# Sums of the first batch's exponentials on TensorE, weight and row stores issued by SyncE and ScalarE, and gate products placed inside the next stage

## The chip, the cores and the metric

The kernel runs on one core of one Trainium2 chip. The time is that of one execution on the device, in microseconds (us), as the median of the runs shown. The profile is of one execution taken by the hardware profiler; a second trace of the changed kernel is compared with it further down.

## What is computed

The reference is an attention with a soft cap, a feed-forward layer, and a mixture of eight experts with capacity routing, in float32:

```python
scores = cap * np.tanh(scale * q @ k.T / cap)             # 4 batches, 12 heads, 448 rows, head size 64
attn   = np.exp(scores - scores.max(-1)); attn /= attn.sum(-1) + 1e-9
x      = attn @ v                                         # 1792 tokens x 768
x      = np.maximum(x @ w_in, 0) ** 2 @ w_out             # 768 -> 2048 -> 768
logits = x @ w_gate                                       # 8 experts
# tokens in falling order of their logits; each expert takes at most 224
out[mask_e] = np.maximum(x[mask_e] @ w1[e], 0) @ w2[e]
```

What this case is about is the sum of the exponentials below the fraction bar, the way of w_in and w_out into the core, and the products with w_gate.

## The kernel before, in words

**Attention** goes batch by batch and, in a batch, by six pairs of heads (`hp`). A pair's exponentials are in four tiles `p`: three of 128 keys for both heads (128x2x448) and one of the last 64 keys of each head (128x448, the upper half for the one head, the lower half for the other). TensorE makes the scores (L230, L232), ScalarE tanh and exp (L234, L235), TensorE the products with `v` (L255, L258). For the denominator GpSimd adds the tiles to one tile `z` (L241, L243, L247 twice), and TensorE sums `z` over its partitions by two products with a tile of ones (`norm`, L263). VectorE adds a small number (L265, for batch 0; ScalarE for the others), takes the reciprocal (L266) and multiplies (L268).

**The feed-forward layer** is three products per tile, since each operand is a high and a low part (`wh`, `wl`, `xh`, `xl`, `gh`, `gl`): `hidden` (L390 to L392) makes 16 tiles per batch, `output` (L440 to L442) six tiles of four weight pieces each. The weights arrive as 64-bit words. For batch 0 a piece is loaded to `raw` (L319, two buffers), decoded by three VectorE instructions (L323, L324, L325) into `wf` (three buffers) and stored to a cache in HBM by GpSimd's queue (L342); later batches load from the cache (L344). `split_weights` makes `wh` on ScalarE (L351) and `wl` on VectorE or GpSimd (L352). `gate_decode` does the same with 24 tiles `wt` of the transposed w_out (store at L486). `finish` transposes a result tile (L418) and stores rows of it (L421); `gate` makes six small products with w_gate (L429), VectorE copies them to `lt` (L460), `logits` transposes that (L475).

**The order.** `merge` takes steps from several generators, always from the one that stands furthest back by the costs that it yields. Stages: attention(0); hidden(0) with attention(1); output(0) and hidden(1) with attention(2); output(1) and hidden(2) with attention(3) and gate_decode; hidden(3) with gate_weights; output(3), output(2), routing and the experts. From the third stage on TensorE's instructions run as they are written. On the other engines the scheduler orders them by its own timeline, so that parts of gate_decode stand well ahead of the stage in which they are written. An instruction that waits holds up all that stand behind it on its engine, and a DMA's issue waits on the issuing engine for the data that it stores. PSUM has two buffers each of `big`, `acc` and `aux`; `aux` serves L255 (`U`), L263, L418, L429 and L475.

## Time and profile before

| | us |
|---|---|
| median of 3 runs (lowest to highest) | 1237.92 (1237.11 to 1242.08) |
| the profiled execution's own time | 1232.37 |
| its span in the trace | 1230.1 |
| TensorE busy | 1113.3 (91%) |
| GpSimd busy | 618.1 (50%) |
| VectorE busy | 680.0 (55%) |

By stage, from windows of the trace (PEclk is the granted TensorE clock, as a share of full speed):

| stage | window, us | TensorE busy | VectorE busy | GpSimd busy | PEclk | DMA share |
|---|---|---|---|---|---|---|
| attention(0) | 5 to 87 | 70.25 of 82 | 56.20 | 50.86 | 0.92 | 0.55 |
| hidden(0), attention(1) | 87 to 194 | 103.69 of 107 | 84.50 | 72.78 | 0.97 | 0.51 |
| output(0), attention(2) | 194 to 307 | 99.71 of 113 | 93.53 | 68.44 | 0.97 | 0.65 |
| hidden(1), end of attention(2) | 307 to 400 | 78.33 of 93 | 69.99 | 29.64 | 0.91 | 0.73 |
| output(1), hidden(2), attention(3) | 400 to 585 | 183.21 of 185 | 85.26 | 50.20 | 1.00 | 0.32 |
| hidden(3), gate_weights | 585 to 660 | 73.84 of 75 | 16.04 | 29.87 | 1.00 | 0.49 |
| output(3) to the experts' end | 660 to 1225 | 504.26 of 565 | 273.42 | 314.21 | 0.92 | 0.42 |

Where TensorE is busy for all of a window at a clock of 1.00, nothing but its own work sets the length. Where it isn't, a wait ended last, and a lower clock beside it makes the work after the wait longer. GpSimd's busy time leaves out the time in which it stands at a DMA's issue.

### The profile page before, as it was taken

How to read it: one execution, taken by the hardware profiler on the slowest of the kernel's cores; microseconds unless marked ns; L12 is line 12 of the kernel's file. 1: busy time of each engine (PE TensorE's matmuls, PEld its weight loads, DVE VectorE, ACT ScalarE, POOL GpSimd, SP SyncE). 2: the span in 40 equal slices, each digit the busy share in tenths (PEclk: the TensorE clock that was granted, in tenths of full speed). 3: DMA queues.
4: the chain of work that ended last, by engine and by line, in shares of the span. 5: the costliest groups of instructions: out<-in, count | busy, mean ns of one | idle time of the engine just before them, and what ended most of it. 6: DMA issues, size and time to landing. Idle time of an engine off the chain costs nothing.

```text
span 1230.1 us, 16798 instructions
## 1 busy us (share of the span) xinstructions
PE 1113.3 (91%) x6170; PEld 869.5 (71%) x6170; DVE 680.0 (55%) x1018; ACT 571.3 (46%) x873; POOL 618.1 (50%) x442
## 2 busy tenths in 40 slices
PE   5899989997797999999999988888797998898997
PEld 1236655665475777677788877777696898898997
DVE  5858879797778534444213446655577763323220
ACT  4787756452374744576563211222232434444542
POOL 4767576665332322222443423436665766766663
PEclk8999989998898999999999987997798988999999
DMA  7433654668777334222651322234344545555551
GB/s 259 151 116 114 213 187 156 211 206 268 265 240 241 112 117 120 90 77 78 205 180 44 101 67 67 76 100 163 121 140 151 159 141 183 193 187 180 191 188 36
DMA packets 70641, 187.35 MB, mean 152 GB/s; under 512 B 8416, under 2 KB 13824, under 8 KB 70560
## 3 DMA queue, kind: packets, MB, share of 16 engines
q1 hardware_dynamic: 55376, 150.48, 38.4%
q0 software_dynamic: 9536, 32.82, 7.4%
q10 hardware_dynamic: 5648, 3.00, 0.9%
q8 instruction: 48, 0.79, 0.2%
q14 instruction: 33, 0.27, 0.1%
HBM read 156.38 MB, written 29.88 MB: 151 GB/s over the span
## 4 chain that ended last, share of the span: by engine, by line
PE 39%; DVE 9%; issue 2%; ACT 1%; POOL 1%; DMA 1%; POOLq 0%; SPq 0%; ACTq 0%; DVEq 0%
PE big L829 9%; PE acc L800 8%; PE acc L440 4%; PE acc L441 3%; PE acc L442 3%; DVE wl L352 3%; PE aux L629 2%; PE acc L390 2%; PE acc L391 2%; PE acc L392 2%; DVE oh L699 2%; PE aux L526 1%; ACT wh L351 1%; PE aux L705 1%; PE acc L746 1%
## 5 line engine op out<-in xcount | busy, mean ns | idle before, releaser
L352 POOL TENSOR_TENSOR wl<-wf,wh 128x768 fp32r<-128x768 f32 (+1 forms) x156 | 268.6, 1725 | 230.5 <-ACT wh L351 227.0
L351 ACT CAST wh<-wf 128x768 fp32r<-128x768 f32 (+1 forms) x238 | 177.8, 747 | 389.4 <-PE acc L441 156.5
L800 PE MATMUL acc<-xs,wh 128*128 128x224 f32 x732 | 143.3, 300 | 32.7 <-DVE gh L816 31.3
L440 PE MATMUL acc<-gh,wh 128*128 128x448 f32 x384 | 158.0, 412 | 0.0
L442 PE MATMUL acc<-gh,wl 128*128 128x448 f32 x384 | 147.0, 383 | 11.2 <-POOL wl L352 10.5
L800 PEld LDWEIGHTS acc<-xs,wh 128*128 128x128 f32 x732 | 124.8, 213 | 36.1 <-DVE gh L816 34.7
L390 PE MATMUL acc<-xh,wh 128*128 128x448 f32 x384 | 147.8, 387 | 0.0
L352 DVE TENSOR_TENSOR wl<-wf,wh 128x768 fp32r<-128x768 f32 (+1 forms) x82 | 96.6, 1178 | 90.8 <-ACT wh L351 90.6
L441 PE MATMUL acc<-gl,wh 128*128 128x448 f32 x384 | 146.6, 382 | 0.0
L391 PE MATMUL acc<-xl,wh 128*128 128x448 f32 x384 | 140.6, 366 | 1.1 <-DVE xl L311 1.1
L392 PE MATMUL acc<-xh,wl 128*128 128x448 f32 x384 | 140.8, 367 | 0.0
L829 PE MATMUL big<-wh,gh 128*112 128x384 f32 x512 | 117.3, 341 | 0.0
L800 PE MATMUL acc<-xs,wl 128*128 128x224 f32 x366 | 107.4, 293 | 0.0
L234 ACT ACTIVATE p<-big,isc 128x896 f32<-128x896 f32 x96 | 86.3, 907 | 39.7 <-PE big L230 34.1
L390 PEld LDWEIGHTS acc<-xh,wh 128*128 128x128 f32 x384 | 72.3, 189 | 35.0 <-issue 19.2
L442 PEld LDWEIGHTS acc<-gh,wl 128*128 128x128 f32 x384 | 76.5, 199 | 21.7 <-POOL wl L352 12.7
L352 POOL TENSOR_TENSOR wl<-raw,wh 128x768 fp32r<-128x768 f32 x37 | 70.0, 1897 | 42.1 <-ACT wh L351 41.8
L235 ACT ACTIVATE p<-p,capt 128x896 f32<-128x896 f32 x96 | 89.7, 949 | 1.6
L440 PEld LDWEIGHTS acc<-gh,wh 128*128 128x128 f32 x384 | 76.6, 200 | 16.4 <-issue 11.0
L829 PEld LDWEIGHTS big<-wh,gh 128*112 128x112 f32 x512 | 86.6, 175 | 0.7
L266 DVE RECIPROCAL d<-d 128x448 f32<-128x448 f32 x24 | 70.8, 2949 | 26.1 <-ACT d L265 25.9
L243 POOL TENSOR_TENSOR z<-z,p 128x896 f32<-128x896 f32 x24 | 51.2, 2133 | 66.2 <-ACT p L235 65.6
(175 smaller groups left out, 1993.6 us busy)
## 6 DMA issues: line engine op xcount, KB each, us to landing
wf<-w SPq DMA_DIRECT2D x78, 384.0 KB, 3.3
raw<-w SPq DMA_DIRECT2D x50, 384.0 KB, 3.2
wf<-wi SPq DMA_DIRECT2D x48, 384.0 KB, 3.1
wf<-wo SPq DMA_DIRECT2D x72, 256.0 KB, 2.6
raw<-w_in SPq DMA_DIRECT2D x16, 768.0 KB, 5.2
raw<-w_out SPq DMA_DIRECT2D x24, 512.0 KB, 3.9
raw<-w_out_t SPq DMA_DIRECT2D x24, 512.0 KB, 4.9
qk<-qk SPq DMA_DIRECT2D x23, 480.0 KB, 5.5
```

The costliest lines, as they stand in the source:

```text
L234: nc.scalar.activation(p, ps[:, :n, :S], AF.Tanh, scale=self.isc)
L235: e = nc.scalar.activation(p, p, AF.Exp, scale=self.capt)
L351: nc.scalar.copy(wh[:, :w], wf[:, :w])
L352: low.tensor_sub(wl[:, :w], wf[:, :w], wh[:, :w].bitcast(F32))
L390: nc.tensor.matmul(ps, wh[:, d], xh, start=(d == 0), stop=False)
L391: nc.tensor.matmul(ps, wh[:, d], xl, start=False, stop=False)
L392: nc.tensor.matmul(ps, wl[:, d], xh, start=False, stop=(d == ND - 1))
L440: nc.tensor.matmul(ps, a, gh, start=(f == 0), stop=False)
L441: nc.tensor.matmul(ps, a, gl, start=False, stop=False)
L442: nc.tensor.matmul(ps, z, gh, start=False, stop=(f == NF - 1))
L800: nc.tensor.matmul(H[j], w[:, d], xs[:, d, x], start=(d == 0 and first), stop=(d == ND - 1 and last))
L829: nc.tensor.matmul(acc[h][:, s, :DM // 2], l, r[:, s * (DM // 2):(s + 1) * (DM // 2)], start=(j == 0 and first), stop=(j == NF2 - 1 and last))
```

## The change

For batch 0 alone GpSimd's additions are gone: `norm` accumulates, per pair of heads, six products with the tile of ones (three tiles, two heads) and one with a new 128x128 tile `duo`, which has ones in its two diagonal 64x64 blocks and so sums the last tile for both heads at once. The weight stores (16 of w_in, 24 of w_out, 24 of its transpose) and the load of `cap` go from GpSimd's queue to SyncE's. The row stores of batches 0 and 1 go from GpSimd's to ScalarE's queue. The gate products, the last tile's `finish` and the logits of batches 0 and 1 are put on a list `tail`, and the next hidden stage runs one of them after each of its first three tiles' products (`trailing`); output(3)'s last `finish` is run in output(2). The copy to `lt` goes to ScalarE, the transposes of `finish` stand behind the second quarter of the next tile's products instead of the first, except in output(2), and in batches 2 and 3 a step is yielded ahead of the last pair's `norm`.

```diff
--- before.py
+++ after.py
@@ -176,10 +176,14 @@
     def setup(self):
         nc, keep = self.nc, self.keep
         capt = keep.tile([128, 1], F32, name="capt")
-        nc.gpsimd.dma_start(capt, bass.AP(tensor=self.capv.tensor, offset=self.capv.offset, ap=[[0, 128], [1, 1]]))
+        nc.sync.dma_start(capt, bass.AP(tensor=self.capv.tensor, offset=self.capv.offset, ap=[[0, 128], [1, 1]]))
         self.capt = capt
         self.ones = keep.tile([128, DH], F32, name="ones")
         nc.vector.memset(self.ones, 1.0)
+        self.duo = keep.tile([128, 128], F32, name="duo")
+        nc.vector.memset(self.duo, 0.0)
+        for h in (slice(0, 64), slice(64, 128)):
+            nc.vector.memset(self.duo[h, h], 1.0)
         self.isc = keep.tile([128, 1], F32, name="isc")
         nc.vector.reciprocal(self.isc, capt)
         nc.vector.tensor_scalar(self.isc, self.isc, DH ** -0.5, None, op0=OP.mult)
@@ -198,6 +202,7 @@
         self.G = {}
         self.loaded = self.ready = 0
         self.x_t = {}
+        self.tail = []
         self.exps, self.norms = [], []
 
     def attention(self, b):
@@ -236,6 +241,8 @@
             if b == 0:
                 self.exps.append(e)
             P[hp, c] = p
+            if b == 0:
+                return
             if c == 1:
                 zs[hp] = z = ap.tile([128, 2, S], F32, name="z", bufs=2)
                 adder.tensor_add(z, P[hp, 0], p)
@@ -259,8 +266,15 @@
 
         def norm(hp):
             z = self.psum.tile([128, S], F32, name="aux")
-            for s in range(2):
-                nc.tensor.matmul(z[s * 64:s * 64 + 64], self.ones, zs[hp][:, s], start=True, stop=True)
+            if b == 0:
+                for c in range(KB):
+                    for s in range(2):
+                        nc.tensor.matmul(z[s * 64:s * 64 + 64], self.ones, P[hp, c][:, s],
+                                         start=(c == 0), stop=False, skip_group_check=True)
+                nc.tensor.matmul(z, self.duo, P[hp, KB][:, 0], start=False, stop=True, skip_group_check=True)
+            else:
+                for s in range(2):
+                    nc.tensor.matmul(z[s * 64:s * 64 + 64], self.ones, zs[hp][:, s], start=True, stop=True)
             d = ap.tile([128, S], F32, name="d", bufs=1)
             (nc.vector.tensor_scalar(d, z, self.eps, None, op0=OP.add) if b == 0 else nc.scalar.activation(d, z, AF.Identity, bias=self.eps))
             nc.vector.reciprocal(d, d)
@@ -290,7 +304,7 @@
                 if not whole:
                     yield 1.6
                 pv(hp - 1, 2, 4)
-                if not whole:
+                if not whole or hp == HP:
                     yield 1.6
                 norm(hp - 1)
                 yield 4.0 if whole else 0.8
@@ -339,7 +353,7 @@
             with self.after(self.norms, WAIT[0], n):
                 self.decode(wf, (self.wi if m == "i" else self.wo)[j], w)
             self.cache[m, j] = self.dram.tile([128, w], F32, name=f"w{m}{j}")
-            nc.gpsimd.dma_start(self.cache[m, j], wf[:, :w])
+            nc.sync.dma_start(self.cache[m, j], wf[:, :w])
         else:
             nc.sync.dma_start(wf[:, :w], self.cache[m, j])
         self.wtile[n] = (wf, w, nc.gpsimd if n >= self.at[NB - 1, "i"] or b == 0 and n % 6 else nc.vector, self.wts, 3)
@@ -392,6 +406,7 @@
                 nc.tensor.matmul(ps, wl[:, d], xh, start=False, stop=(d == ND - 1))
                 if d == 2:
                     yield 1.7
+            yield from self.trailing()
             r = mp.tile([128, S], F32, name="r", bufs=2)
             nc.scalar.activation(r, ps, AF.Relu)
             nc.scalar.activation(r, r, AF.Square)
@@ -402,6 +417,12 @@
             G.append((gh, gl))
             yield 1.7
 
+    def trailing(self):
+
+        if self.tail:
+            self.tail.pop(0)()
+            yield 1.5
+
     def output(self, b):
         nc, mp = self.nc, self.mp
         base = self.at[b, "o"]
@@ -418,7 +439,7 @@
                 nc.tensor.transpose(ps[:, c], xt[:, c * KP:(c + 1) * KP], self.c("ident"))
             o = mp.tile([KP, KC, 128], F32, name="rows", bufs=2)
             (nc.vector.tensor_copy if b == LAST and j == ND - 1 else nc.scalar.copy)(o, ps)
-            (nc.gpsimd if gated else nc.scalar).dma_start(
+            nc.scalar.dma_start(
                 rows[j // DA][b, :, :, j % DA * 128:(j % DA + 1) * 128], o)
             if b == LAST:
                 self.stored = j + 1
@@ -447,20 +468,29 @@
                         yield None
                     self.load_experts(-1)
                     yield from self.feed(0, 0)
-                if q == 0 and last is not None:
+                if q == int(b != LAST) and last is not None:
                     finish(*last)
                     yield 1.4
+                if j == 0:
+                    yield from self.trailing()
             xt = self.tp.tile([128, S], F32, name="xt")
             (nc.vector.tensor_copy if b == LAST and j == ND - 1 else nc.scalar.copy)(xt, ps)
             xts.append(xt)
             last = (j, xt)
-        if gated:
+        def gates():
+            nonlocal pl
             pl = self.psum.tile([128, S], F32, name="aux")
             gate(0, ND)
-            nc.vector.tensor_copy(lt, pl)
-            self.logits(b)
-        finish(*last)
-        yield 2.5
+            nc.scalar.copy(lt, pl)
+
+        pl = None
+        if gated:
+            self.tail += [gates, lambda: finish(*last), lambda: self.logits(b)]
+        elif b != LAST:
+            self.tail.append(lambda: finish(*last))
+        else:
+            finish(*last)
+            yield 2.5
 
     def gate_half(self, b):
         if b % 2 == 0:
@@ -483,7 +513,7 @@
             t = self.ap.tile([128, 512], F32, name="wt", bufs=2)
             self.decode(t, self.wot[i], 512)
             self.cache["t", i] = self.dram.tile([128, 512], F32, name=f"wt{i}")
-            self.nc.gpsimd.dma_start(self.cache["t", i], t)
+            self.nc.sync.dma_start(self.cache["t", i], t)
             yield 1.0
 
     def gate_weights(self):
```

The order changes at three places. First TensorE, in the first pair of heads; `aux_151` and `aux_148` are the products with `v`, `aux_159` and `aux_156` the denominators. Before:

```order
L255 MATMUL aux_151<-p2_122,v_99 64x448 x2
L230 MATMUL big_143<-qk_97 128x448 x2
L258 MATMUL aux_151<-p1_128,v_99 128x448
L263 MATMUL aux_159<-z_117,ones_68 64x448 x2
L230 MATMUL big_167<-qk_97 128x448 x2
L232 MATMUL big_174<-qk_97 128x448
L255 MATMUL aux_199<-p2_140,v_103 64x448 x2
L255 MATMUL aux_199<-p2_146,v_103 64x448 x2
L230 MATMUL big_185<-qk_101 128x448 x2
```

And of the change:

```order
L262 MATMUL aux_148<-p2_124,v_103 64x448 x2
L272 MATMUL aux_156<-p2_124,ones_68 64x448 x2
L235 MATMUL big_142<-qk_101 128x448 x2
L265 MATMUL aux_148<-p1_129,v_103 128x448
L274 MATMUL aux_156<-p1_129,duo_70 128x448
L235 MATMUL big_169<-qk_101 128x448 x2
L237 MATMUL big_175<-qk_101 128x448
L262 MATMUL aux_196<-p2_139,v_107 64x448 x2
L262 MATMUL aux_196<-p2_145,v_107 64x448 x2
L235 MATMUL big_184<-qk_105 128x448 x2
L235 MATMUL big_190<-qk_105 128x448 x2
```

The last product of the denominator follows the last one with `v` directly, where the two products over `z` stood; the first six stand beside the products with `v` that read the same tiles.

Second GpSimd, at the end of attention(2), beside hidden(1): `z_2419` are the sums of batch 2's last pair, `wt15` to `wt21` stores of decoded tiles of the transposed w_out. Before:

```order
L241 TENSOR_TENSOR z_2419<-p2_2410,p2_2416 128x896
L486 DMA wt15_3698<-wt_3692 128x512
L486 DMA wt16_3770<-wt_3764 128x512
L486 DMA wt17_3826<-wt_3820 128x512
L486 DMA wt18_3880<-wt_3874 128x512
L486 DMA wt19_3950<-wt_3944 128x512
L243 TENSOR_TENSOR z_2419<-z_2419,p2_2584 128x896
L486 DMA wt20_4022<-wt_4016 128x512
L247 TENSOR_TENSOR z_2419<-z_2419,p1_2590 64x448 x2
L486 DMA wt21_4078<-wt_4072 128x512
```

Of the change, with the same pair's sums as `z_2407` and the next batch's first ones as `z_2869`:

```order
L248 TENSOR_TENSOR z_2215<-p2_2206,p2_2212 128x896
L250 TENSOR_TENSOR z_2215<-z_2215,p2_2352 128x896
L254 TENSOR_TENSOR z_2215<-z_2215,p1_2358 64x448 x2
L248 TENSOR_TENSOR z_2407<-p2_2398,p2_2404 128x896
L250 TENSOR_TENSOR z_2407<-z_2407,p2_2572 128x896
L254 TENSOR_TENSOR z_2407<-z_2407,p1_2578 64x448 x2
L248 TENSOR_TENSOR z_2869<-p2_2860,p2_2866 128x896
```

And SyncE of the change where output(0) ends, with `wo23`, `wt0` and `wt1` as stores, and the cached loads of hidden(1) (`wi0` to `wi2`) behind them:

```order
L333 DMA raw_2872<-w_out_t 128x512
L356 DMA wo23_2072<-wf_2066 128x512
L333 DMA raw_2918<-w_out_t 128x512
L516 DMA wt0_2877<-wt_2871 128x512
L333 DMA raw_2980<-w_out_t 128x512
L358 DMA wf_2090<-wi0_421 128x768
L224 DMA v_2201<-v 128x512
L516 DMA wt1_2923<-wt_2917 128x512
L333 DMA raw_3043<-w_out_t 128x512
L358 DMA wf_2116<-wi1_433 128x768
L358 DMA wf_2134<-wi2_445 128x768
```

GpSimd keeps the three sums of each pair and nothing between them; each store stands on SyncE just ahead of the raw load that is two tiles further on.

Third TensorE, where output(0) ends and hidden(1) begins. Before:

```order
L440 MATMUL acc<-gh,wh 128x448
L441 MATMUL acc<-gl,wh 128x448
L442 MATMUL acc<-gh,wl 128x448
L429 MATMUL aux<-xt,wgt 32x448 x6
L475 MATMUL aux<-cf,lt 128x128 x3
L418 MATMUL aux<-cf,xt 112x128 x4
L230 MATMUL big<-qk 128x448 x4
L390 MATMUL acc<-xh,wh 128x448
```

Of the change, the six gate products behind the last of the 18 products of hidden(1)'s first tile:

```order
L404 MATMUL acc<-xh,wh 128x448
L405 MATMUL acc<-xl,wh 128x448
L406 MATMUL acc<-xh,wl 128x448
L450 MATMUL aux<-xt,wgt 32x448 x6
L235 MATMUL big<-qk 128x448 x4
```

and further on, behind the second and the third tile, the transposes of the last result tile and those of the logits:

```order
L262 MATMUL aux<-p_1986,v 64x448 x2
L262 MATMUL aux<-p_2149,v 64x448 x2
L265 MATMUL aux<-p_2155,v 128x448
L277 MATMUL aux<-z,ones 64x448 x2
...
L406 MATMUL acc<-xh,wl 128x448
L439 MATMUL aux<-cf,xt 112x128 x4
L404 MATMUL acc<-xh,wh 128x448
...
L406 MATMUL acc<-xh,wl 128x448
L505 MATMUL aux<-cf,lt 128x128 x3
L404 MATMUL acc<-xh,wh 128x448
```

Between the gate products and the transposes of `lt` there was nothing; now two tiles of hidden(1) and a pair of attention(2) stand between them.

## Rows read from the trace of the kernel before

**Rows 1.** The page: the engines' busy time.

```profile
PE 1113.3 (91%) x6170; PEld 869.5 (71%) x6170; DVE 680.0 (55%) x1018; ACT 571.3 (46%) x873; POOL 618.1 (50%) x442
```

**Rows 2.** Waits, 100 to 420 us: engine, line, releaser: us, times, longest.

```profile
POOL wt L486 <- DVE wt L325: 67.4, 20, 8.2
...
POOL wo L342 <- DVE wf L325: 27.2, 16, 2.7
...
PE aux L263 <- POOL z L247: 11.2, 4, 6.9
...
PE acc L442 <- POOL wl L352: 10.5, 6, 3.7
...
DVE wf L323 <- DMA raw<-w_out: 9.0, 8, 2.7
...
PE aux L475 <- DVE lt L460: 7.2, 1, 7.2
```

**Rows 3.** Waits of TensorE alone, 5 to 95 us.

```profile
PE aux L263 <- POOL z L247: 7.2, 1, 7.2
...
PE aux L255 <- DVE d L265: 4.2, 2, 2.5
```

**Rows 4.** Windows: length, five engines' busy us, PEclk, DMA share, GB/s.

```profile
5.00:87.00 82.00, 70.25 (x242) 24.14 (x244) 56.20 (x45) 54.93 (x65) 50.86 (x34) 0.92 0.55 185
20.00:30.00 10.00, 6.58 (x12) 1.70 (x14) 8.54 (x7) 1.02 (x2) 6.17 (x5) 0.54 0.90 300
160.00:170.00 10.00, 10.00 (x33) 6.47 (x33) 5.79 (x7) 6.12 (x10) 6.38 (x5) 0.71 0.61 190
310.00:320.00 10.00, 2.96 (x11) 2.19 (x13) 8.46 (x9) 0.58 (x1) 6.39 (x6) 0.63 0.65 230
```

**Rows 5.** Timeline, first pair of heads; columns: start us, us, instruction, idle before.

```profile
21.47 0.56 DVE L323 TENSOR_SCALAR wf<-raw 128x768 int32<-128x768 int32 x1 [0.29 <-DMA raw<-w_in]
...
23.36 3.57 PE L263 MATMUL aux<-z,ones 128*64 128x448 f32 x4 [7.25 <-POOL z L247]
...
26.97 0.69 DVE L265 TENSOR_SCALAR d<-aux,eps 128x448 f32<-128x448 f32 x1 [1.03 <-PE aux L263]
...
29.88 1.35 PE L255 MATMUL aux<-p,v 128*64 128x448 f32 x6
```

**Rows 6.** Timeline of TensorE, back-to-back attention products.

```profile
67.05 2.48 PE L255 MATMUL aux<-p,v 128*64 128x448 f32 x12
...
69.46 1.02 PE L230 MATMUL big<-qk 64*128 64x448 f32 x4
...
70.41 1.02 PE L258 MATMUL aux<-p,v 128*128 128x448 f32 x2
```

**Rows 7.** Timeline of GpSimd and TensorE, last pair of batch 2.

```profile
380.95 0.54 POOL L486 DMA_DIRECT2D wt<-wt  x1 [4.07 <-DVE wt L325]
...
386.42 2.62 POOL L247 TENSOR_TENSOR z<-z,p 64x448 f32<-64x448 f32 x2
...
387.61 3.24 PE L263 MATMUL aux<-z,ones 128*64 128x448 f32 x4 [6.94 <-POOL z L247]
```

**Rows 8.** Timeline, gate products after the output stages of batches 0 and 1.

```profile
306.68 1.69 PE L429 MATMUL aux<-xt,wgt 128*32 128x448 f32 x10
...
316.37 0.61 DVE L460 COPY lt<-aux 128x448 f32<-128x448 f32 x1
...
317.04 0.90 PE L475 MATMUL aux<-cf,lt 128*128 128x128 f32 x3 [7.21 <-DVE lt L460]
...
502.48 0.66 PE L475 MATMUL aux<-cf,lt 128*128 128x128 f32 x4 [0.94 <-DVE lt L460]
```

**Rows 9.** DMA issues: transfer, queue, count, KB each, median us to landing.

```profile
raw<-w_out SPq DMA_DIRECT2D x24, 512.0 KB, 3.9
...
wf<-wo SPq DMA_DIRECT2D x72, 256.0 KB, 2.6
```

**Rows 10.** Waits of SyncE's issues, 100 to 420 us.

```profile
SPq L319 <- DVE wf L325: 141.8, 29, 12.3
```

## The prediction

> **What bounds the kernel now.** I read first the busy times on the page, then the windows by stage, then TensorE's waits, and last the timeline around the longest of them. TensorE is the bound: 1113.3 us busy of a span of 1230.1 [rows 1]. The table by stage shows where it isn't full: attention(0), output(0) and hidden(1), with 70.25 of 82, 99.71 of 113 and 78.33 of 93 us. The stages after, to 660 us, are full at a clock of 1.00, and the change leaves what comes after them as it was, so whatever it is worth has to come out of the first 400 us.
>
> There TensorE waits from 100 to 420 us for GpSimd's sums `z` (11.2 us), for low parts `wl` that GpSimd makes (10.5) and once for the copy `lt` (7.2), 28.9 us together [rows 2]; from 5 to 95 us for `z` (7.2) and for VectorE's `d` (4.2) [rows 3]. Behind the first two is GpSimd, which stands 67.4 and 27.2 us at stores whose tile VectorE hasn't decoded [rows 2]; sums and low parts queue behind. The last pair of batch 2 shows it: a store waits 4.07 us to 380.95, the second last sum can start only then, a second store comes between, the last sum begins at 386.42, and TensorE waits 6.94 [rows 7]. Each such wait costs twice, since the granted clock after it is lower: 0.71 from 160 to 170, 0.63 from 310 to 320, 0.54 from 20 to 30 [rows 4], that is, between 1.2 and 2.4 GHz for part of the window.
>
> **The change part by part.** All terms are on the scale of the profiled execution, 1232.37, which lies 5.55 below the median of the runs shown, 1237.92; the result is moved by that at the end.
>
> *First batch's sums.* A pair gets six half products, which take 2.41 us (the twelve entries from 67.05 to the next start at 69.46), and one over `duo`, of the shape of the L258 that takes 1.02; it loses two half products, a third of 2.41, or 0.80 [rows 6]. That is 2.63 us a pair, 15.8 for six, all of it on TensorE. Against this stand 11.75 us in which TensorE is idle from 5 to 87 [rows 4], nearly all of it the waits of 7.2 and 4.2 [rows 3], and the slow clock: from 20 to 30, 6.58 busy us at 0.54 [rows 4] are 3.6 at full speed, so 3 go, and I allow 1 elsewhere. Then the stage needs 70.25 + 15.8 − 4 = 82 without any wait, as long as it is now. The wait for `z` goes, since the products need only the exponentials. What is late next is `d`: in VectorE's order it stands behind the third weight tile's decode, which starts at 21.47, after its load; today `d` starts at 26.97 and the next pair's products at 29.88 [rows 5]. I leave 2 of the 4.2 us of waits for `d`. Result +2. Bounds: −1, if the products fill gaps only, and +15.8, if they hide nowhere.
>
> *Stores off GpSimd, hidden(0) with attention(1).* Of the 11.2 us for `z`, 6.9 are batch 2's last pair, so 4.3 are three waits further ahead [rows 2]; the clock of 0.71 from 160 to 170 costs 2.9 [rows 4]. Up to −7.2; GpSimd also makes five of six low parts there, which don't vanish: −5.
>
> *Output(0).* The 10.5 us for `wl` [rows 2], and 0.03 of 113 us in clock (3.4): up to −14. But VectorE, busy 93.53 of 113, decodes here, and eight times it waits for a raw load itself, 9.0 us [rows 2]. A decode, not the store, may be what ends last once GpSimd is free. Between 0 and −14 I take −5.
>
> *Gate products and logits.* Now six products, 7.21 us of wait for the copy that VectorE makes at 316.37 behind a decode, then the transposes [rows 8]. After the change ScalarE copies, and two tiles of hidden(1) and a pair's attention products lie between. The 7.2 go; the window from 310 to 320 holds 2.96 us of products at 0.63 [rows 4], so some 1.1 there and a little either side. −9, from 0 (if the tile's own weights come late instead) to −10. After batch 1 the same step waits 0.94 [rows 8]; with the 0.5 beside it −1.5.
>
> *Last pair of batch 2.* 6.94 us of wait, and 3.24 for four entries that take 1.02 elsewhere [rows 6, 7]: 9.1 at most, −8 with a little left for the sums, which still take 2.62 for the last step.
>
> *At no cost:* twelve issues on ScalarE, some 0.54 each if they are as GpSimd's [rows 7], and the copy to `lt` (0.61 on VectorE [rows 8]). ScalarE is 46% busy [rows 1]; if none of it hides, +7. The store of a tile on SyncE's queue becomes ready with the end of the same decode that frees the raw buffer for the load behind it, so that it adds a wait for nothing new, only its issue and its bytes.
>
> Sum: 2 − 5 − 5 − 9 − 1.5 − 8 = −26.5, so 1205.9, and 1211.4 by the median. With the favourable ends (−1, −7.2, −14, −10, −1.5, −9.1) −43, or 1195; with the poor ends of the terms whose cover is doubtful (+15.8, 0, 0, −5, 0, −4) +6.8, or 1245.
>
> **The rivals.**
>
> *First batch dearer, output(0) kept by decodes.* The products fall at the full 15.8 and output(0) gives nothing: −26.5 + 13.8 + 5 = −7.7, 1230.2. For it: attention(0) would need all its 82 us for TensorE's work, so a wait that stays comes on top; VectorE is 83% busy in output(0). Against it: 11.4 us of the stage are waits that depend on GpSimd or on what comes after it. With half of it, 1226.
>
> *Stores delay the raw loads.* This is the slower side. In the new order each store stands on SyncE just ahead of the raw load two tiles on, and hidden(1)'s cached loads stand behind both. A raw load of 512 KB takes 3.9 us, a load of 256 KB 2.6 [rows 9], so 256 KB more in the same queue may put 1.3 us on each of 24 loads, 31 us; with two raw buffers half of that is hidden, 16 in output(0), and 16 again for the transposed tiles in hidden(1). Then 2 − 5 + 16 − 9 + 16 − 8 − 1.5 = +10.5, 1248.4; it decides from about 0.75 us a load. For it: VectorE already waits for eight of these loads, and the DMA share is 0.65 and 0.73 in these stages. Against it: the same bytes moved before, beside the loads, and SyncE's raw loads stood 141.8 us waiting for decodes [rows 10], so the loads have slack. The Trainium skill, page "DMA: Bandwidth & Descriptors", section "Queues, rings and completion order", says that a DMA engine takes turns between queue rows packet by packet, which would make the own queue of GpSimd's stores a protection that is now lost; no row here shows that.
>
> *Only the issue time is saved.* If the work behind the stores would be as late without them, since it is VectorE's decodes that hold the `p`, `wh` and `wf` buffers and not GpSimd's place in line, then hidden(0), output(0) and the last pair give nothing: −26.5 + 18 = −8.5, 1229.4. For it: GpSimd waits for VectorE, and VectorE remains. Against it: rows 7 show sums whose operands were there while the store stood before them. The Trainium skill, page "DMA: Bandwidth & Descriptors", section "Issuing engines are not separate DMA queues", says that issuing DMAs from several engines saves only the sequencer's time to initiate them, usually small; by it alone this rival would be the forecast. The trace differs: an issue takes 0.54 us, and the wait ahead of it 4.07.
>
> **How the numbers follow.** Within 0.5%, or 6.2 us (1231.7 to 1244.1), a measurement of this kernel can't tell a difference from no change. The forecast, 1211, with its own range of 1196 to 1222: 0.66. A gain beyond that: 0.04. The first rival, 1224 to 1238: 0.16, of which 0.10 faster and 0.06 the same. Only the issue time, 1229: 0.06, of which 0.03 and 0.02, and 0.01 slower. The delayed raw loads, 1248: 0.08, of which 0.02 the same. So faster 0.83, same 0.10, slower 0.07. The range, 1196 to 1235, holds the forecast and most of the first and third case and leaves out about 0.15.
>
> **What would show it.** In the profile of the changed kernel: no row of GpSimd waiting at a store; the waits of 28.9 us from 100 to 420 shrunk below 8; a clock of 1.00 where 0.71 and 0.63 stand; attention(0) ending within 3 us of where it does now, with its idle time below 3. Wrong would make it: raw loads for which VectorE waits well over 9 us, with `wl` or `wh` late behind them; attention(0) longer by 10 us; TensorE waiting in hidden(1)'s first tile for weights that the gates' place used to hide; or a new wait at `d`.

## The result, and the profile after

| | before | after |
|---|---|---|
| median, us | 1237.51 (4 runs, 1232.89 to 1242.08) | 1202.83 (4 runs, 1201.22 to 1203.80) |
| profiled execution, us | 1232.37 | 1202.53 |
| span, us | 1230.1 | 1200.4 |

The ratio is 0.9719, with an interval of 0.9681 to 0.9756: 34.7 us faster by the medians, where 26.5 was forecast, and the time lies in the range that was forecast. A second measurement of the same kernel beside other runs gave 0.9678 (0.9635 to 0.9720). The profiled execution before lay 5 us under its median and the one after on it, so that the spans differ by 29.7 only.

TensorE's waits after the change, the first line from 5 to 95 us and the others from 100 to 420, and two of VectorE's (line waited at, releaser: us, times, longest), against [rows 2, 3]:

```profile
PE aux L262 <- DVE d L279: 2.1, 2, 1.8
...
DVE wt L337 <- DMA raw<-w_out_t: 19.8, 14, 2.9
...
PE acc L406 <- DVE wl L366: 10.0, 3, 5.0
...
DVE wf L337 <- DMA raw<-w_out: 8.7, 7, 3.5
...
PE acc L404 <- ACT wh L365: 2.7, 1, 2.7
...
PE aux L277 <- DVE x L282: 2.1, 1, 2.1
```

The waits for `z` (7.2 and 11.2) are gone, so is that of 10.5 for GpSimd's `wl` in output(0) and that of 7.2 for `lt`. Of the 4.2 for `d` 2.1 are left. New are 10.0 and 2.7 for `wl` and `wh` at L406 and L404, the products of a hidden stage. No row of GpSimd at a store is left. VectorE's 19.8 for raw loads of the transposed tiles were 4.0 before, beside 21.7 for the landing of stores of such tiles, which are gone; the runs further down come back to both.

By windows, with the columns of [rows 4]; the first block is of the change, for attention(0), its first pair, output(0) and the stretch from there to output(1):

```profile
5.00:87.00 82.00, 78.30 (x316) 29.03 (x316) 44.93 (x43) 56.83 (x67) 8.93 (x5) 1.00 0.54 192
20.00:30.00 10.00, 8.18 (x38) 2.79 (x38) 7.27 (x7) 6.10 (x8) 0.00 (x0) 1.00 0.99 360
185.28:280.66 95.38, 93.47 (x425) 65.01 (x423) 83.10 (x85) 46.29 (x68) 54.68 (x32) 1.00 0.62 218
280.66:382.64 101.98, 88.26 (x390) 64.13 (x390) 82.22 (x109) 58.61 (x92) 19.98 (x11) 0.92 0.79 269
```

and of the kernel before, for the last two of these:

```profile
194.09:306.75 112.66, 99.37 (x429) 66.61 (x431) 93.44 (x98) 51.21 (x74) 68.35 (x65) 0.97 0.65 214
306.75:409.20 102.45, 87.78 (x390) 63.29 (x390) 74.82 (x102) 55.35 (x88) 30.01 (x32) 0.92 0.71 242
```

From 5 to 87 and from 20 to 30 the clock is 1.00 where 0.92 and 0.54 stood. Output(0) takes 95.38 us where it took 112.66, with the same products: TensorE's idle time fell from 13.3 to 1.9, and its busy time by 5.9, at a clock of 1.00 for 0.97. The stretch behind it, with hidden(1) in it, was 102.45 and is 101.98, though its two big waits have gone. So a forecast of −5 for the first and −17 for the second came out as −17.3 and −0.5.

The timeline of TensorE, VectorE and ScalarE where hidden(1) begins and a few tiles on (start, us, instruction, idle time before):

```profile
282.49 0.83 ACT L365 CAST wh<-wf 128x768 fp32r<-128x768 f32 x1 [8.06 <-DMA wf<-wi]
...
283.37 0.65 PE L404 MATMUL acc<-xh,wh 128*128 128x448 f32 x1 [2.71 <-ACT wh L365]
...
286.77 0.95 DVE L366 TENSOR_TENSOR wl<-wf,wh 128x768 fp32r<-128x768 f32 x1
...
287.78 0.74 PE L406 MATMUL acc<-xh,wl 128*128 128x448 f32 x1 [3.38 <-DVE wl L366]
...
293.93 1.70 PE L450 MATMUL aux<-xt,wgt 128*32 128x448 f32 x12
...
309.56 0.49 PE L505 MATMUL aux<-cf,lt 128*128 128x128 f32 x3
...
343.96 2.94 DVE L280 RECIPROCAL d<-d 128x448 f32<-128x448 f32 x1
...
346.82 0.90 DVE L366 TENSOR_TENSOR wl<-wf,wh 128x768 fp32r<-128x768 f32 x1
...
347.77 0.74 PE L406 MATMUL acc<-xh,wl 128*128 128x448 f32 x1 [4.99 <-DVE wl L366]
```

Hidden(1)'s first products wait for the cast of their weights, whose load ScalarE has waited 8.06 us for; then for `wl`, which VectorE makes at 286.77, among the steps of w_out_t decodes; only then come the gates, and `lt` is transposed without a wait at 309.56. Sixty us on `wl` is late again, by 4.99, with a reciprocal of 2.94 and a decode ahead of it on VectorE.

How far each mark of the program is moved, in us against the trace before (each from the start or end of one product in the trace). A second trace of the changed kernel, that of change_again, has each mark from output(0) on within 1.5 us of the first one:

| mark | before, at | after |
|---|---|---|
| last product with `v` of the first batch's last pair | 80.8 | −2.4 |
| first product of hidden(0)'s sixth tile | 114.8 | −6.4 |
| first product of output(0) | 194.1 | −8.8 |
| last product of output(0) | 306.8 | −26.1 |
| first product of output(1) | 409.2 | −26.6 |
| first product of output(3) | 658.6 | −30.2 |
| first product of the experts | 866.9 | −36.2 |
| end | 1222.1 | −29.8 |

### The profile page after: what moved, and what is told of

It is laid out like the page before. It is cut to its first block, busy times and chain, and to the rows that moved or that the text cites. A ratio compares the mean times of both kernels' runs of the same rounds, so it can differ in the third digit from the quotient of the medians.

```text
span 1200.4 us, 16789 instructions
## 1 busy us (share of the span) xinstructions
PE 1108.5 (92%) x6230; PEld 871.1 (73%) x6230; DVE 669.2 (56%) x1019; ACT 570.9 (48%) x875; POOL 545.0 (45%) x341
## 4 chain that ended last, share of the span: by engine, by line
PE 61%; DVE 20%; DMA 7%; issue 7%; ACT 2%; POOL 2%; SPq 0%; POOLq 0%; DVEq 0%; ACTq 0%
PE acc L830 9%; PE big L859 8%; PE acc L461 6%; PE acc L462 5%; PE acc L463 5%; PE acc L404 4%; PE acc L406 4%; PE acc L405 4%; DVE wl L366 3%; DMA raw<-w_out 3%; PE big L235 3%; PE aux L262 3%; DVE wf L338 3%; DVE wf L337 2%; PE aux L659 2%
## 5 line engine op out<-in xcount | busy, mean ns | idle before, releaser
L366 POOL TENSOR_TENSOR wl<-wf,wh 128x768 fp32r<-128x768 f32 (+1 forms) x156 | 278.8, 1790 | 315.8 <-ACT wh L365 308.9
L404 PE MATMUL acc<-xh,wh 128*128 128x448 f32 x384 | 151.7, 395 | 3.6 <-ACT wh L365 2.7
L406 PE MATMUL acc<-xh,wl 128*128 128x448 f32 x384 | 142.7, 372 | 10.1 <-DVE wl L366 10.0
L250 POOL TENSOR_TENSOR z<-z,p 128x896 f32<-128x896 f32 x18 | 39.0, 2164 | 159.2 <-ACT p L240 158.3
L404 PEld LDWEIGHTS acc<-xh,wh 128*128 128x128 f32 x384 | 72.9, 190 | 36.3 <-issue 19.4
L406 PEld LDWEIGHTS acc<-xh,wl 128*128 128x128 f32 x384 | 73.2, 191 | 21.9 <-DVE wl L366 11.9
L461 PEld LDWEIGHTS acc<-gh,wh 128*128 128x128 f32 x384 | 76.2, 199 | 14.6 <-issue 9.6
```

What stands on the lines that cost most here:

```text
L366: low.tensor_sub(wl[:, :w], wf[:, :w], wh[:, :w].bitcast(F32))
L404: nc.tensor.matmul(ps, wh[:, d], xh, start=(d == 0), stop=False)
L406: nc.tensor.matmul(ps, wl[:, d], xh, start=False, stop=(d == ND - 1))
L461: nc.tensor.matmul(ps, a, gh, start=(f == 0), stop=False)
```

## The experiments

Theory A: what cost was GpSimd standing at stores, with the first batch's sums nearly free. Its rivals are told in the expectations. Each run was timed against the kernel before; the mark tables below go by their traces.

**The parts by themselves.** The edit of each is the part of the diff above that its name says; `no_tail` is the sums and the stores together.

```diff
 sums_only:   + duo, six products with ones and one with duo for batch 0; - three GpSimd additions
 stores_only: - nc.gpsimd.dma_start   + nc.sync.dma_start (wi, wo, wt, capt), nc.scalar.dma_start (rows)
 tail_only:   + self.tail, trailing(); lt copied by ScalarE; finish at q == 1;
                the yield ahead of norm at hp == HP
 no_tail:     sums_only and stores_only
```

> The kernel before, with the first batch's sums on TensorE and nothing else of the change. Theory A (the stores in GpSimd's queue are what costs; the sums are nearly free because the first stage's waits pay for them): attention(0) ends 2 to 3 us earlier, the rest is as before, 1234 to 1236, ratio 0.997 to 0.999. Rival B (the gain in output(0) comes from a GpSimd that enters the second stage without arrears from the first batch's sums): a third of the gain or more, 1226 or below.

Measured: 1235.06, ratio 0.9961 (0.9945 to 0.9978).

> The kernel before, with the weight, row and cap transfers moved off GpSimd's queue and nothing else. Theory A: hidden(0) -5, output(0) -17, last pair of batch 2 -9; the 7.2 us for the logits stay, and hidden(1)'s first weights arrive behind them: -31, 1206, ratio 0.975. Rival C (the terms add up as forecast: hidden(0) -5, output(0) -5, last pair -8): -18, 1219, ratio 0.985.

Measured: 1221.96, 0.9862 (0.9821 to 0.9902).

> The kernel before, with only the gate products, last result tile and logits put into the next hidden stage (and the copy on ScalarE). Theory A: the 7.2 us for the copy go, but hidden(1)'s weights come late in their place, so half is left, -5 to -3, 1233 to 1235. Rival C (as forecast): gates -9 and -1.5, 1227, ratio 0.991.

Measured: 1217.15, 0.9809 (0.9774 to 0.9844).

> The kernel before with the sums and the stores, without the part on gate products: the change less that part. Theory A: the wait for the logits is back and the wait for hidden(1)'s weights is gone, so that it is about as fast as the change: 1203 to 1207, ratio 0.973 to 0.976. Rival C (the gate part is worth its 10.5): 1213, ratio 0.980.

Measured: 1215.55, 0.9793 (0.9755 to 0.9830).

| mark, us against before | sums_only | stores_only | tail_only | no_tail | the change |
|---|---|---|---|---|---|
| first of output(0) | −2.6 | −2.4 | −1.7 | −8.8 | −8.8 |
| last of output(0) | −9.0 | −18.0 | −3.4 | −24.6 | −26.1 |
| first of output(1) | −2.7 | −16.8 | −12.3 | −21.8 | −26.6 |
| first of output(3) | −2.1 | −15.9 | −15.8 | −21.5 | −30.2 |
| first of the experts | −1.7 | −16.4 | −21.8 | −21.7 | −36.2 |

The sums came as theory A has it by the time, if a little better by the ratio (0.9961 for 0.997 to 0.999). The other three missed it: it had stores_only at 1206, tail_only at 1233 to 1235, no_tail at 1203 to 1207. Rival C was near for no_tail (1213), and tail_only was faster than either had it (1227 by rival C). By the total stores_only was near rival C too (1219), but not by the marks: output(0) is 15.6 shorter there, three times the forecast, and the stretch behind it gives 1.2 back. Its waits from 100 to 420 show why:

```profile
PE aux L429 <- ACT xt L454: 6.2, 1, 6.2
...
PE aux L475 <- DVE lt L460: 4.9, 1, 4.9
```

The gate products wait for ScalarE's `xt` and `lt` waits for VectorE, where the last pair's sums waited before. In tail_only these are gone and another stands there:

```profile
PE acc L393 <- DVE wl L353: 7.2, 2, 4.4
```

Of what is gained ahead of hidden(1) a part is lost in it: sums_only reaches the end of output(0) 9.0 us earlier and output(1) 2.7, no_tail 24.6 and 21.8. By the medians the three parts alone give −4.8, −17.9 and −22.7, 45.4 us, and together 34.7. So something in that stretch may have a pace of its own, which the later runs test.

**The first batch's sums, once more.** The edit is the change less the sums: these lines of `scores` go, and with them `duo` and the branch of `norm` for batch 0.

```diff
-            if b == 0:
-                return
...
```

> The change without the first batch's sums (these are GpSimd's again). Theory A, with what the parts alone have shown: the sums are worth 6 us beside the stores (1222.0 less 1215.6), so 1207 to 1210, ratio 0.976. Rival (the price that was forecast, the sums cost 2): 1200 to 1202, ratio 0.970.

Measured: 1206.84, 0.9749 (0.9704 to 0.9794): theory A, 4 to 6 us against the change, though by intervals that overlap; in its trace output(0) begins at 191.9, 6.6 us later than with the change. What the sums free is GpSimd, and with it VectorE. VectorE's second decode instruction to 90 us, in the kernel before and in sums_only (mean ns after the comma):

```profile
L324 DVE SCALAR_TENSOR_TENSOR wf<-raw,wf 128x768 int32<-128x768 int32 x6 | 12.8, 2125 | 0.2
```

```profile
L337 DVE SCALAR_TENSOR_TENSOR wf<-raw,wf 128x768 int32<-128x768 int32 x6 | 5.8, 959 | 0.2
```

and VectorE and GpSimd in the kernel before, in the first pair:

```profile
14.43 0.96 DVE L324 SCALAR_TENSOR_TENSOR wf<-raw,wf 128x768 int32<-128x768 int32 x1
...
16.89 3.29 DVE L324 SCALAR_TENSOR_TENSOR wf<-raw,wf 128x768 int32<-128x768 int32 x1
...
17.27 2.09 POOL L243 TENSOR_TENSOR z<-z,p 128x896 f32<-128x896 f32 x1
```

The same instruction takes 0.96 us alone (2125 in the mean beside the sums), and 3.29 when a GpSimd addition of 2.09 begins while it runs. Without the additions VectorE is busy for 44.93 us of the first 82, not 56.20. The Trainium skill, page "SBUF — State Buffer", section "SBUF: two separate sides", describes a port pair that VectorE, with two inputs in SBUF, and GpSimd lock against one another: the first to start has it for its whole instruction, and the other is blocked. The trace agrees in the size, with 2.33 us lost beside an addition of 2.09, but not in the order: by the records VectorE started first, at 16.89 for 17.27, and lost.

**Which stores.** The kernel before, with L342 alone on SyncE:

```diff
-            nc.gpsimd.dma_start(self.cache[m, j], wf[:, :w])
+            nc.sync.dma_start(self.cache[m, j], wf[:, :w])
```

> The kernel before, with only the stores of the decoded w_in and w_out tiles on SyncE; row stores and w_out_t stores stay on GpSimd. Theory A (output(0) was held by GpSimd standing at these stores): output(0) 14 to 18 us shorter, the last pair of batch 2 waits for its sums as before, 1224 to 1228. Rival F (it is the row stores or the w_out_t stores that stand at the end of output(0)): output(0) at most 6 shorter, 1233 or more.

Measured: 1229.14, 0.9918 (0.9886 to 0.9949), a little over what theory A had. Output(0) is 13.8 us shorter (−2.4 at its first product, −16.2 at its last), the last pair's wait of 6.9 stands:

```profile
PE aux L263 <- POOL z L247: 6.9, 1, 6.9
```

So 13.8 of the 15.6 us that all stores give in output(0) are the w_in and w_out stores. Rival F falls. Another rival was not named: such stores also land sooner from SyncE's queue (those of w_out in 2.3 us at the median in stores_only, 4.7 before), and so give their buffers back sooner. The trace before speaks against it, since from 194 to 307 us VectorE waits for such a landing once only:

```profile
DVE wf L323 <- DMA wo<-wf: 0.3, 1, 0.3
```

**What paces hidden(1).** Theory D: the 24 w_out_t decodes, which the scheduler draws into one burst from output(0)'s end on. Rival E: the stores ahead of the loads on SyncE's queue, the mechanism of the slower side in the prediction. The change, with L516 back on GpSimd:

```diff
-            self.nc.sync.dma_start(self.cache["t", i], t)
+            self.nc.gpsimd.dma_start(self.cache["t", i], t)
```

> The change with the 24 stores of decoded w_out_t tiles back on GpSimd's queue. Theory D (hidden(1)'s new waits for wh and wl are VectorE's and the loads' pace with the w_out_t decodes): they stay, 6 to 13 us, and the waits for the sums come back, about 9: 1208 to 1213. Rival E (the stores on SyncE's queue put the cached loads of hidden(1) late): the waits for wh and wl go, those for the sums come: 1199 to 1204.

Measured: 1200.60, 0.9678 (0.9643 to 0.9713). Neither fits in full. The time is in E's window and the wait for `wh` is gone, but a wait of 4.9 for `wl` stays in hidden(1) and one of 6.5 for GpSimd's `wl` appears in output(0):

```profile
PE acc L463 <- POOL wl L366: 6.5, 1, 6.5
PE acc L406 <- DVE wl L366: 4.9, 1, 4.9
```

And output(1) begins at 382.62, with the change at 382.64. TensorE waits elsewhere and is through at the same time, as a burst with a pace of its own would have it.

**The burst moved.** All 24 decodes held back behind hidden(1), that is, behind its last subtraction for `gl`:

```diff
-            (nc.gpsimd if b == 0 and j % 3 == 0 else nc.vector).tensor_sub(gl, r, gh.bitcast(F32))
+            self.sub = (nc.gpsimd if b == 0 and j % 3 == 0 else nc.vector).tensor_sub(gl, r, gh.bitcast(F32))
...
+        mark = self.sub.ins
         for i in range(ND * 4):
...
-            self.decode(t, self.wot[i], 512)
+            with self.tc.issue_after(mark):
+                self.decode(t, self.wot[i], 512)
```

> The change with the decoding of the w_out_t tiles held back until hidden(1)'s last tile is through VectorE; they then lie beside output(1) and hidden(2), where the DMA share is 0.38 and VectorE under half busy. Theory D and rival E both: the waits of hidden(1) for wh and wl, 13 us with those at its first tile, shrink below 4, output(1) begins 8 to 12 us earlier, 1191 to 1196. Rival G (hidden(1) is held by the cached loads themselves or by the sums): output(1) begins as with the change, 1200 or more. If the decodes collide with output(1) instead, the same gain is lost there.

Measured: 1200.17, 0.9687 (0.9654 to 0.9720); its trace is of an execution 6 us under that median. Hidden(1)'s stretch, from output(0)'s last product at 281.89, and output(1) as far as its last product:

```profile
281.89:364.55 82.66, 82.65 (x391) 60.96 (x390) 42.42 (x43) 57.69 (x92) 20.50 (x11) 1.00 0.37 113
364.55:470.38 105.83, 95.70 (x420) 69.12 (x419) 78.77 (x104) 49.93 (x74) 24.88 (x13) 0.94 0.77 256
```

The stretch takes 82.66 us with TensorE full, 19.3 less than with the change, and output(1) 105.83 in place of 89.2. The collision that the last sentence of the expectation names came in full, with a wait of its own:

```profile
PE acc L463 <- DVE wl L366: 10.1, 3, 4.3
```

Output(1) begins 18 us earlier than with the change, not 8 to 12, and ends 1.4 earlier. From the first to the last step of these decodes on VectorE it is 109.0 us in the kernel before (290.6 to 399.5), 106.0 with the change (273.8 to 379.8), 107.9 with the stores on GpSimd and 107.4 here (369.0 to 476.4): 4.4 to 4.5 us a tile, whichever stage lies beside it (101 to 111 us in all the kernels here that don't spread the decodes). That is longer than the 82 and 89 us that TensorE needs for these stages. Rival G falls, and so does E as the main cause, since 4.5 us a tile stood before the change too, with the stores on another queue.

What the pace is made of shows in VectorE's waits between output(0)'s last product and output(1)'s first, with the change and before it:

```profile
DVE wt L337 <- DMA raw<-w_out_t: 18.8, 13, 2.9
```

```profile
DVE wt L323 <- DMA wt<-wt: 21.7, 11, 3.8
...
DVE wt L323 <- DMA raw<-w_out_t: 1.9, 3, 1.2
```

With the change VectorE is busy for 82.22 of these 101.98 us and waits for raw loads in nearly all of the rest; before, 74.82 of 102.45, and mostly the landing of a store ended its waits. So it is VectorE that has no slack there, and the new queue changed what it waits for and hardly how long.

**The burst spread.** Each decode held back behind the low part that the program made last before it, on the change, the same with the stores on GpSimd, and on the kernel before:

```diff
-        low.tensor_sub(wl[:, :w], wf[:, :w], wh[:, :w].bitcast(F32))
+        self.sub = low.tensor_sub(wl[:, :w], wf[:, :w], wh[:, :w].bitcast(F32))
...
-            self.decode(t, self.wot[i], 512)
+            with self.tc.issue_after(self.sub.ins):
+                self.decode(t, self.wot[i], 512)
```

> The change itself, beside the two kernels below, so that they can be compared on one chip: ratio 0.968 to 0.976.

Measured: 1200.57, 0.9678 (0.9635 to 0.9720).

> The change with each w_out_t decode held back until the low part that the program made last before it, so that the 24 decodes are spread over output(1) and hidden(2) and not in a burst. Theory D (what holds hidden(1), or output(1) when all are moved behind hidden(1), is the burst of decodes on VectorE and of raw loads): output(1) begins 16 to 18 us earlier than with the change and keeps at least 10 of it to its end: 1187 to 1193, ratio 0.958 to 0.963. Rival H (each decode costs its time to TensorE wherever it stands, some 0.7 us): the gain is given back as when they were all behind hidden(1), 1199 to 1203.

Measured: 1179.68, 0.9527 (0.9486 to 0.9569), better than theory D had it, 20.9 us under the change in the same comparison. Rival H falls: output(1) keeps its 89.2 us.

> As wt_paced, with the 24 stores of w_out_t tiles on GpSimd's queue. If a store that waits for a decode is what holds GpSimd's sums and low parts up, 3 to 10 us longer than wt_paced; if spread decodes leave GpSimd no wait that matters, within 2 us of it.

Measured: 1182.77, 0.9555 (0.9517 to 0.9592): 3.1 us over wt_paced, with intervals that overlap; left open.

> The kernel before, with each w_out_t decode held back as in wt_paced and nothing of the change; the stores stay on GpSimd. Theory D (the wait of 6.9 us for the last pair's sums and that of 7.2 for the logits in hidden(1) are the burst of decodes, on GpSimd's stores and on VectorE): both shrink below 2, output(0) stays within 6 us of its length before, output(1) begins 14 to 18 us earlier, 1220 to 1226, ratio 0.984 to 0.990. Rival I (the place of the gate products and the queue of the stores cause these waits, whatever the pace): at least 10 of the 14 us stay, 1233 or more.

Measured: 1217.63, 0.9831 (0.9814 to 0.9848): below the window by 2.4, on theory D's side, with output(1) 21.0 us earlier; its decodes are spread over 156.7 us. The windows of output(0), hidden(1)'s stretch and output(1) in wt_paced, and of the first two in before_paced:

```profile
184.11:279.76 95.65, 93.46 (x426) 65.35 (x425) 81.48 (x81) 47.60 (x70) 51.89 (x32) 1.00 0.65 220
279.76:362.01 82.25, 82.25 (x390) 60.96 (x389) 42.31 (x43) 57.69 (x92) 20.51 (x11) 1.00 0.38 113
362.01:451.20 89.19, 89.19 (x420) 64.52 (x419) 67.92 (x78) 49.96 (x74) 23.32 (x13) 1.00 0.72 229
```

```profile
192.15:302.84 110.69, 100.37 (x429) 66.13 (x431) 87.22 (x86) 51.20 (x74) 66.90 (x62) 0.95 0.66 207
302.84:388.18 85.34, 83.56 (x389) 61.56 (x390) 41.10 (x42) 55.34 (x88) 20.42 (x12) 1.00 0.32 96
```

| us | before | change | wt_on_gpsimd | wt_late | wt_paced | before_paced |
|---|---|---|---|---|---|---|
| output(0) | 112.7 | 95.4 | 104.7 | 95.0 | 95.6 | 110.7 |
| from there to output(1) | 102.4 | 102.0 | 91.5 | 82.7 | 82.2 | 85.3 |
| output(1) | 89.2 | 89.2 | 89.2 | 105.8 | 89.2 | 89.2 |

Pacing alone takes 17.1 us from the kernel before in the middle stretch and 2.0 in output(0); the change takes 17.3 in output(0) and 0.5 in the middle. The two don't overlap, and wt_paced has both. By its median it is the fastest of these kernels.

## Why the prediction was right, and which of its steps were not

It was right in direction and size, but the size is in part luck: the terms of the sum were off by −5.8, −12.3, +16.5, −2.1, −6.0 and +6.4 us in the order of the table, and these errors cancel to −3.3.

| term of the sum | forecast | measured (marks) |
|---|---|---|
| first batch's sums, and hidden(0) with attention(1) | +2 − 5 | −8.8 |
| output(0) | −5 | −17.3 |
| gate products, and last pair of batch 2 | −9 − 8 | −0.5 |
| output(1) to output(3) | −1.5 | −3.6 |
| output(3) and output(2) | 0 | −6.0 |
| experts | 0 | +6.4 |
| sum, on the traces | −26.5 | −29.8 |

*First batch.* The gross price was right: 15.3 us busy for the 36 half products and 5.6 for the six over `duo` (each shown as two entries), 20.9, where six times 2.41 + 1.02 is 20.6. So were the 2 us of waits for `d` that were left. What was mis-sized is the credit, "it loses two half products, a third of 2.41, or 0.80", 4.8 for six pairs. From 5 to 87 us, the products over `z` before, and two pairs of them by themselves, then the new products:

```profile
L263 PE MATMUL aux<-z,ones 128*64 128x448 f32 x24 | 11.2, 634 | 7.3 <-POOL z L247 7.2
```

```profile
36.04 0.97 PE L263 MATMUL aux<-z,ones 128*64 128x448 f32 x2
...
63.04 0.97 PE L263 MATMUL aux<-z,ones 128*64 128x448 f32 x4
```

```profile
L272 PE MATMUL aux<-p,ones 128*64 128x448 f32 x72 | 15.3, 545 | 0.0
...
L274 PE MATMUL aux<-p,duo 128*128 128x448 f32 x12 | 5.6, 548 | 0.0
```

Both half products took 0.97 us where they stood side by side, but each one took that where they stood apart, as in three of the six pairs, and the first pair's took 3.57 at the slow clock [rows 5]: 11.2 in all. So up to the last product with `v` TensorE's busy time rose by 5.6 us, where 15.8 − 4 was forecast, and its idle time fell by 8.1, from 11.75 to 3.7, where 9.75 was: −2.4, not +2. Behind it the gain grows to 6.4 at hidden(0)'s sixth tile, 5.5 with the sums alone. VectorE, freed of GpSimd's additions, is busy for 11 us less in the stage, most of it in the decode, which the sum left out; that this is what brings hidden(0)'s tiles earlier is argued and not shown by a run of its own. That the decode's second instruction took 2125 ns in the mean there and 0.96 us by itself stood in the trace before. By output(0) the sums alone give 2.6 and the stores alone 2.4, both together 8.8.

*Output(0).* The step that failed is "A decode, not the store, may be what ends last once GpSimd is free." VectorE's waits for raw loads stayed, 8.7 for 9.0, and TensorE is idle for 1.9 us in all; wo_stores_only by itself, with 7.4 us of these waits, makes the stage 13.8 shorter. The bound of 14 was passed too, for the slow clock had been priced at 3.4 and TensorE's busy time fell by 5.9.

*Gate products and last pair.* Both waits went, as forecast, and nothing was gained. The bound of zero had its reason, "if the tile's own weights come late instead", and the last section named the wait; the value was chosen by the size of the wait that goes, not by what paces the stage. In before_paced TensorE is idle for 1.8 us in this stretch, with the gates and the stores where they were (0.9 of it for `lt`): the cause of both waits was the burst. The part on gates is worth its 9 only where the burst leaves room: in tail_only, where output(0) ends 14.6 us after the burst's begin (6.9 with the change), hidden(1)'s third tile begins 11.6 us sooner after output(0)'s end than before, and 2.7 of that are lost again by output(1).

*Behind 660 us* the statement that the change leaves everything as it was failed. All kernels with the tail part reach the experts 6 to 12 us sooner relative to output(3)'s first product, and those without it within 0.5; the moved `finish` of output(3) is in this part. Which wait pays was not taken apart, and routing's instructions lie in the same stretch. The experts' +6.4 is no cost of the change: kernels that alter nothing there show it too, no_tail +6.5, sums_only +3.5, before_paced +3.0. The trace before was a short one in this stage, which may also answer for most of its 5 us under the median.

*The rivals.* The first was wrong in both halves. The slower one, raw loads delayed by stores on SyncE's queue, did not come as a cost: a w_out raw load takes 4.1 us at the median in stores_only, 3.9 before [rows 9], not 1.3 more, and wo_stores_only is faster with just these stores moved. Some of its signs did come, and with them two of the prediction's signs of being wrong: VectorE waits 19.8 us for raw loads of the transposed tiles, and hidden(1)'s first tile waits 2.71 for `wh`, whose load was late, and 3.38 for `wl`. But these waits stand in place of others, and output(1) begins at the same time with the 24 stores back on GpSimd's queue. Of the signs of being right, TensorE's idle time in attention(0) is 3.7 and not below 3, and the clock behind output(0) is still 0.92. "Only the issue time is saved" is refuted by wo_stores_only, in which output(0) is 13.8 us shorter though SyncE issues the same 40 stores behind the same decodes. The Trainium skill, page "DMA: Bandwidth & Descriptors", section "Issuing engines are not separate DMA queues", has the transfers share the same DMA engines whichever engine issues them, and the runs do not speak against that; its "usually small" saving is what these runs show to be larger, since an engine that stands at an issue keeps its own work waiting.

## What to carry to other kernels

A wait that goes is worth at most the distance to the next thing that paces its stage; so look for a chain of loads and decodes that has a length of its own (here 24 tiles at 4.4 to 4.5 us, with VectorE busy or waiting for their transfers nearly throughout) before pricing the waits inside it one by one. If such a chain is not needed soon, spread it: on this kernel and on the one before that was worth 20 us, for two lines. An in-order engine with work that others wait for should issue no transfer that waits for a third engine.

## What the runs showed of the hardware that was not expected

A VectorE instruction with two operands in SBUF took 0.96 us alone and up to 3.29 beside a GpSimd addition of 2.09, 2.125 in the mean of the first batch. Where two half products stood apart each took TensorE 0.97 us, as long as both together.

The 64 stores added to SyncE's queue hardly lengthened its loads. The kernel before, then stores_only, whose trace shows the landing of all these transfers (KB each, median us to landing):

```profile
raw<-w_out_t SPq DMA_DIRECT2D x24, 512.0 KB, 4.9
...
wo<-wf POOLq DMA_DIRECT2D x24, 256.0 KB, 4.7
```

```profile
raw<-w_out SPq DMA_DIRECT2D x24, 512.0 KB, 4.1
raw<-w_out_t SPq DMA_DIRECT2D x24, 512.0 KB, 4.5
...
wo<-wf SPq DMA_DIRECT2D x24, 256.0 KB, 2.3
```

The loads of w_out went from 3.9 [rows 9] to 4.1 us, those of the transposed tiles from 4.9 to 4.5, and the stores of w_out themselves from 4.7 to 2.3.
